# Score products of a pair of units issued in two halves, with the weight transposes of the preceding unit between them

## The chip, the core and the metric

The kernel runs on one core of a Trainium2 chip. The metric is the device time of one execution in microseconds (us); three runs of the kernel before gave a median of 644.97 us (644.82 to 645.6). One more execution was profiled, and all rows below come from it.

A core has five engines that run their own instruction queues and meet through semaphores: TensorE (PE in the rows; PEld is its weight load), VectorE (DVE), ScalarE (ACT), GpSimd (POOL) and SyncE (SP), which here only issues DMAs. Each queue is in order.

## The reference

Three stages follow each other. This case changes the first one alone.

1. Attention over 4 batches, 8 heads of 64, 512 local tokens and 32 global ones. A local query sees the 32 global keys and the local keys within 32 positions; a global query sees all.

```python
s_ll = np.where(np.abs(pos[:, None] - pos[None, :]) <= 32, scale * q_l @ k_l.T, -1e9)
a_l  = sm(np.concatenate([scale * q_l @ k_g.T, s_ll], axis=-1))   # row-wise softmax
out_l = a_l @ np.concatenate([v_g, v_l])
out_g = sm(scale * q_g @ k_all.T) @ v_all
```

2. A mixture of 8 experts (512 to 1024 to 512) over the 2304 resulting tokens, one expert a token. The choice is serial along a sequence: a token takes its own best expert, or the one of the token before, by a gate computed from the token.
3. A gated feed-forward layer with a convolution of three taps along the sequence.

## The kernel before, in words

The attention runs over 32 units `n`, in the order batch `b`, quarter `i` of the local queries (128 tokens), half `g` of the heads (4 heads). An even unit and the odd one behind it are a pair: they share the batch and the tokens and differ in the half of the heads. Code is written out by hand in program order (`manual_schedule`): each engine executes what the Python loop emits for it, in that order. The steps of a unit are spread over several turns of the loop (`Attn.run`, L459 on):

- `s_mm` (L247), at even units only, for both units of the pair: eight mask products (L259, bf16), then 32 score products (L267, in the order of the four heads `hp`, four windows `c`, two halves). They use a quarter-width, half-height part of the array each (64x32), and each is two matmuls in the trace, 64 a pair. The results are two tiles `sp`, one for each unit.
- `softmax` (L271): a reduction to the row's minimum on DVE (L275, `nm`), then four exponentials on ACT (L278, `pr`). The reduction needs the whole `sp` of its unit.
- `pt` (L281), one turn later: four 128x128 transposes of `pr` on PE (L286, `ptp`, a PSUM tile of the ring `tr`), and a copy on ACT (L288, `pts`), which frees the PSUM tile.
- `pv_norm` (L448), two turns later: 32 products with V on PE (L300; 128x32), and at odd units the division by the sum on DVE and the store.

The names of the tiles around them: `trp` (L173) are transposes of the next batch's keys and queries, `trx` (L319) transposes of the finished tokens for the logits, `sa`, `sb`, `ptg`, `og` (L368, L389, L399) the same steps for the global queries. All names beginning with `r_` belong to the routing of the experts, which VectorE works on from unit 21 on. `trp`, `ptp`, `trx`, `ptg` and `sb` share the three PSUM buffers `tr`: a fourth one waits until the first has been copied away.

In a turn of the loop the emission is: `s_mm` (even units), `softmax`, the transposes and copies for the next batch, `pt` of the unit before, `x_t`, `pv_norm` of the unit two before, logits, the steps of the global queries. Behind the attention comes the tail of the routing (to about 180 us), then the experts and the feed-forward stage, each with its products queued on PE in program order.

Of the kernel before, what the change touches and what calls it, by code (L numbers as in the profile page):

```python
# [87 lines left out]
class Attn:  # L88
# [158 lines left out]
    def s_mm(self, n):  # L247
        b, i, _ = n
        nc = self.nc
        qT, kT = self.qT[b % 2], self.kT[b % 2]  # L250
        sp = [self.psS.tile([P, 4, P], F32, tag="S", name="sp") for _ in range(2)]
        rows = [slice(64 * g, 64 * g + 64) for g in range(2)]
        for c in range(4):
            u = 4 * i + c
            edge = u in (0, 15)
            t = u // 15 if edge else (u - 1) % 3
            for g, r in enumerate(rows):
                o = 64 * g + 32 * edge
                nc.tensor.matmul(sp[g][32 * c:32 * c + 32], self.identb[r, o:o + 32],  # L259
                                 self.masks[r, t, None, :].to_broadcast([64, 4, P]), start=True, stop=False)  # L260
        for hp in range(4):
            for c in range(4):
                u = 4 * i + c
                v = u - 1
                s0 = 4 * (v // 3) + (0, 2, 3)[v % 3] + 1
                for g, r in enumerate(rows):
                    nc.tensor.matmul(sp[g][32 * c:32 * c + 32, hp, :], qT[r, hp, 32 * u:32 * u + 32],  # L267
                                     kT[r, hp, s0:s0 + 4, :], start=False, stop=hp == 3)
        return sp

    def softmax(self, n, sp):  # L271
        b, i, g = n
# [137 lines left out]
    def run(self):  # L410
        nc = self.nc
        units = [(b, i, g) for b in range(B) for i in range(4) for g in range(2)]
        N = len(units)
        pr, pts, ops, xs, xts, gst = {}, {}, {}, {}, {}, {}
        self.alloc(0)
        for a in range(4):
            self.load_qk(0, 1, a)
            self.load_qk(0, 0, a)
        self.load_gn(0)
        self.load_g(0)  # L420
        self.load_v(0, range(2))
        self.alloc(1)
        for a in range(N_K1):
            self.load_qk(1, 1, a)
        self.warm(NWARM)
        arr = {1: nc.vector.tensor_copy, 0: nc.scalar.copy}
        for a in range(5):
            for t in (1, 0):
                if a < 4:
                    self.arrange_a(0, t, a, arr[t])  # L430
            for t in (1, 0):
                if a > 0:
                    self.tr_all(0, t, a - 1, "tr")
        self.tr_g(0)
        self.warm(NWARM_G)
        eng = {"a": nc.scalar.copy, "p": nc.gpsimd.tensor_copy, "v": nc.vector.tensor_copy}
        glob, vcopy = self.copy_v(0, (0, 2), (0, 1), (0, 2), True)
        for e, j in zip(E_VG, glob):
            eng[e](*j)
        self.load_v(0, range(2, 6))  # L440
        self.copy_v(0, (2, 4), (1, 3), (2, 4))
        self.copy_v(0, (4, 6), (3, 5), (4, 6))
        for a in range(N_K1, 4):
            self.load_qk(1, 1, a)
        self.load_qk(1, 0)
        self.load_g(1)

        def pv_norm(n):  # L448
            b, i, g = units[n]
            if g == 0:  # L450
                ops[0] = self.ps1.tile([P, 2, 512], F32, tag="O", name="op")
            self.pv(units[n], pts.pop(n), ops[0])
            if g == 1:
                xf = self.norm(ops[0])
                t0 = b * S + SG + 128 * i
                nc.sync.dma_start(self.x_dram[t0:t0 + 128, :], xf)
                xs[n] = xf

        for n in range(N):  # L459
            b, i, g = units[n]  # L460
            m = n % 8
            self.n = n
            if g == 0:
                sps = self.s_mm(units[n])
            sp = sps[g]
            if n == N - 1:
                pts[n - 1] = self.pt(units[n - 1], pr.pop(n - 1))
            tr = []
            if b + 1 < B:
                pc = nc.gpsimd.tensor_copy  # L470
                ars, trs, mg = ARS[b > 0], TRS[b > 0], MG[b > 0]
                tr = list(trs.get(m, ()))
            if n in Q_EARLY:
                while tr and tr[0] > 3:
                    self.tr_all(b + 1, 0, tr.pop(0) - 4)
            pr[n] = self.softmax(units[n], sp)
            if n == 1:
                for e, j in zip(E_VC, vcopy):
                    eng[e](*j)
            next(self.late, None)  # L480
            self.hook(n, 0)
            if b + 1 < B:
                if m == mg:
                    self.tr_g(b + 1)
                for st in tr:
                    self.tr_all(b + 1, 1 - st // 4, st % 4)
                for st in ars.get(m, ()):
                    self.arrange_a(b + 1, 1 - st // 4, st % 4, pc if b else nc.scalar.copy)
                for a in LD_Q[b].get(m, ()):
                    self.load_qk(b + 1, 0, a)  # L490
                if 2 <= m < 5:
                    self.load_v(b + 1, range(2 * m - 4, 2 * m - 2))
                if m == (5 if b == 0 else 2) and b + 2 < B:
                    self.alloc(b + 2)
                    self.load_g(b + 2)
                if b + 2 < B:
                    for t in (1, 0):
                        for a in PF[b > 0][t].get(m, ()):
                            self.load_qk(b + 2, t, a)
                if m == 3:  # L500
                    self.copy_v(b + 1, (0, 3), (0, 3), (0, 3))
                if m == 4:
                    self.copy_v(b + 1, (3, 6), (3, 5), (3, 6))
            self.copy_some(V_JOBS[min(b, 2)].get(m, 0))
            self.warm(WARM.get(n, 0))
            if 0 < n < N - 1:
                pts[n - 1] = self.pt(units[n - 1], pr.pop(n - 1))
            if n - 3 in xs:
                b, i, g = units[n - 3]
                xts[i] = self.x_t(xs.pop(n - 3))  # L510
            if n >= 2:
                pv_norm(n - 2)
            if 0 <= n - 4 and (n - 4) % 8 == 7:
                self.logits([xts[i] for i in range(4)], units[n - 4][0])
            if n == 19:
                self.logits([self.x_t(xg, 64)], 4, 64)
            if 0 <= n - 5 < N - 1 and (n - 5) % 8 == 7:
                self.evac(units[n - 5][0], self.ps, "tr")
                if n == 20:
                    self.evac(4, self.ps, "tr", 64)  # L520
            b, i, g = units[n]
            m = n % 8
            for gg in range(2):
                st = m - ((3 + 2 * gg) if b == 0 else (2 if b < 3 else 0) + 3 * gg)
                if st == 0:
                    gst[gg] = self.sg_softmax(b, gg, *self.sg_mm(b, gg))
                if st == 1:
                    gst[gg, "p"] = self.sg_pt(gst[gg])
                if st == 2:
                    self.sg_pv(b, gg, gst[gg, "p"])  # L530
            if n == 8:
                self.c2.close()
            if n == 17:
                xg = self.load_xg(range(2))
            if b == 3 and m == 6:
                xg = self.load_xg(range(B))
            self.hook(n, 1)
        hk = iter(range(N, N + 9))
        pv_norm(N - 2)
        xt = self.x_t(xg)  # L540
        pts[N - 1] = self.pt(units[N - 1], pr.pop(N - 1))
        self.hook(next(hk), 1)
        xts[2] = self.x_t(xs.pop(N - 3))
        pv_norm(N - 1)
        self.hook(next(hk), 1)
        self.logits([xt], 4)
        self.hook(next(hk), 1)
        xts[3] = self.x_t(xs.pop(N - 1))
        self.evac(4, self.ps, "tr")
        t = self.ps.tile([P, P], F32, tag="tr", name="lgp")  # L550
        self.logit_mm(t, xts, range(3))
        self.hook(next(hk), 1)
        self.logit_mm(t, xts, (3,))
        self.logit_out(t, 3)
        self.hook(next(hk), 1)
        self.evac(3, self.ps, "tr")
# [1166 lines left out]
```

## Time and profile before

| | |
|---|---|
| median of 3 runs | 644.97 us |
| the profiled execution | 645.35 us, of which the span from the first to the last instruction is 643.6 us |
| PE busy | 604.7 us, 94% of the span |
| PEld / DVE / ACT / POOL busy | 508.0 / 418.8 / 320.9 / 174.7 us |
| granted TensorE clock | 0.995 of 2.4 GHz over the span |
| the units of the attention | about 12 to 142 us of the span |

The busy times are sums over the whole span. In the views of a stretch, a row of the timeline is a run of like instructions: its start, its length, the engine, the line, the operation, the tiles with their shapes, how many (x), and in brackets how long the engine had been idle before and what ended that. "issue" stands for an idle time for which the trace shows no other engine. Matmuls are pipelined: the length of one matmul (0.27 us) is longer than the distance between the starts of two.

### The profile page before, as it was taken

The page shows a single profiled execution, that of the slowest core. Times are in us where ns is not written, and L with a number is a line of the kernel's source. Part 1 is how long each engine was busy: PE and PEld are TensorE (multiplying, and loading weights), DVE is VectorE, ACT ScalarE, POOL GpSimd, SP SyncE. Part 2 cuts the span into 40 slices and gives each one's busy share as a digit, 9 for nine tenths or more (in the row PEclk, how much of TensorE's full clock was granted, in tenths as well). Part 3 has the DMA queues.
Part 4 walks back from the last instruction along what each step waited for, and adds up shares of the span by engine and source line. Part 5 has one row for each costly group of instructions (what it writes and reads, how often), then busy time and mean ns, then how long its engine had stood idle before and what let it go on. Part 6 is the DMA issues. An engine that isn't in the chain of part 4 may idle for free. (4 is left out here: it accounts for less than half of the span.)

```text
span 643.6 us, 15270 instructions
## 1 busy us (share of the span) xinstructions
PE 604.7 (94%) x5898; PEld 508.0 (79%) x5898; DVE 418.8 (65%) x874; ACT 320.9 (50%) x629; POOL 174.7 (27%) x226
## 2 busy tenths in 40 slices
PE   8888898888999999999999999987999999999997
PEld 7666676665778888888888888857998898898986
DVE  7877577958836676875778677586893393393340
ACT  4754555573225546352454634664874374373331
POOL 7664810070212232423222251000042042300200
PEclk9999999999999999999999999997999999999999
DMA  9999668652158454953545494023101201000001
GB/s 226 217 244 236 177 142 209 240 168 75 55 201 314 140 182 171 344 207 132 211 143 184 145 347 157 16 86 88 31 20 49 68 16 50 34 1 34 34 34 49
DMA packets 60089, 88.12 MB, mean 137 GB/s; under 512 B 25710, under 2 KB 34182, under 8 KB 59976
## 3 DMA queue, kind: packets, MB, share of 16 engines
q1 hardware_dynamic: 56488, 76.83, 38.3%
q0 software_dynamic: 3520, 10.23, 4.6%
q8 instruction: 48, 0.79, 0.5%
q14 instruction: 33, 0.27, 0.1%
HBM read 125.87 MB, written 15.79 MB: 220 GB/s over the span
## 5 line engine op out<-in xcount | busy, mean ns | idle before, releaser
L1433 DVE SCALAR_TENSOR_TENSOR fc<-f_hp,cw,fc 128x544 f32<-128x544 f32 (+2 forms) x66 | 51.4, 778 | 71.5 <-ACT fc L1431 70.0
L1027 DVE TENSOR_TENSOR wl<-ws,wh 128x512 fp32r<-128x512 f32 (+1 forms) x92 | 71.8, 848 | 5.3 <-ACT wh L1026 5.2
L1106 PE MATMUL yp<-wh,gh 128*128 128x512 f32 x176 | 71.0, 404 | 1.1 <-ACTq L1277 0.9
L1106 PE MATMUL yp<-wl,gh 128*128 128x512 f32 x176 | 69.0, 392 | 0.7 <-DVEq L1277 0.7
L1106 PE MATMUL yp<-wh,gl 128*128 128x512 f32 x176 | 69.1, 393 | 0.0
L1026 ACT CAST wh<-ws 128x512 fp32r<-128x512 f32 (+1 forms) x96 | 66.1, 779 | 0.0
L1255 ACT ACTIVATE hs<-hp 128x512 f32<-128x512 f32 x44 | 24.3, 595 | 74.2 <-PE hp L1090 74.1
L1090 PE MATMUL hp<-wh,xh 128*128 128x512 f32 x176 | 58.6, 405 | 0.7 <-ACT xh L1079 0.7
L1090 PE MATMUL hp<-wl,xh 128*128 128x512 f32 x176 | 56.2, 392 | 0.0
L1090 PE MATMUL hp<-wh,xl 128*128 128x512 f32 x176 | 56.0, 391 | 0.0
L1491 PE MATMUL f<-wh,fh 128*128 128x512 f32 (+1 forms) x144 | 55.5, 385 | 0.0
L1491 PE MATMUL f<-wl,fh 128*128 128x512 f32 (+1 forms) x144 | 55.0, 382 | 0.0
L1491 PE MATMUL f<-wh,fl 128*128 128x512 f32 (+1 forms) x144 | 55.0, 382 | 0.0
L1063 POOL DMA_INDIRECT y_dram<-ys,sidx x22 | 24.6, 1118 | 105.7 <-ACT ys L1259 88.9
L1083 DVE TENSOR_TENSOR gl<-hlp,gh 128x512 fp32r<-128x512 f32 x44 | 28.4, 686 | 32.4 <-ACT gh L1079 32.3
L278 ACT ACTIVATE pr<-sp,nm 128x128 f32<-128x128 f32 x128 | 36.6, 376 | 25.7 <-DVE nm L275 25.7
L999 POOL TENSOR_TENSOR wf<-wf,fx 128x512 int32<-128x512 int32 x16 | 20.8, 1303 | 100.9 <-DVE fx L998 100.9
L1259 ACT COPY ys<-yp 128x512 f32<-128x512 f32 x22 | 12.9, 587 | 61.2 <-PE yp L1106 56.5
L1051 POOL DMA_INDIRECT xs<-x_dram,gidx x22 | 27.5, 1249 | 45.5 <-ACT pr L278 34.0
L1106 PEld LDWEIGHTS yp<-wh,gh 128*128 128x128 f32 x176 | 33.1, 188 | 7.7 <-ACTq L1277 1.1
L1090 PEld LDWEIGHTS hp<-wl,xh 128*128 128x128 f32 x176 | 32.9, 188 | 7.8 <-DVE wl L1027 0.9
L1106 PEld LDWEIGHTS yp<-wh,gl 128*128 128x128 f32 x176 | 33.0, 188 | 7.6 <-DVE gl L1083 0.6
(357 smaller groups left out, 1492.5 us busy)
## 6 DMA issues: line engine op xcount, KB each, us to landing
ws<-in_moe_w_dram SPq DMA_DIRECT2D x42, 2048.0 KB
fx<-y_dram SPq DMA_DIRECT2D x17, 256.0 KB
raw<-in_k_l_dram SPq DMA_DIRECT2D x16, 256.0 KB
x_dram<-x SPq DMA_DIRECT2D x16, 256.0 KB
fx<-in_moe_w_in_dram SPq DMA_DIRECT2D x8, 512.0 KB
fx<-in_moe_w_out_dram SPq DMA_DIRECT2D x8, 512.0 KB
out_dram<-fy SPq DMA_DIRECT2D x16, 256.0 KB
VA<-in_v_l_dram SPq DMA_DIRECT2D x20, 192.0 KB
```

The lines of the kernel that those rows point to most:

```text
L278: nc.scalar.activation(pr[:, hp, :], sp[:, hp, :], AF.Exp, bias=nm[:, hp:hp + 1], scale=-1.0)
L999: nc.gpsimd.tensor_tensor(a, a, lo, ALU.add)
L1026: (cp.tensor_copy if cp else self.nc.scalar.copy)(h, src[n][:, k, :])
L1027: eng.tensor_tensor(l, src[n][:, k, :], h.bitcast(F32), ALU.subtract)
L1051: self.nc.gpsimd.indirect_dma_start(out=xs, out_offset=None, in_=self.x_dram[0:n, :], in_offset=bass.IndirectOffsetOnAxis(ap=self.rt.gidx[ ...
L1063: self.nc.gpsimd.indirect_dma_start(out=self.y_dram[:, :], out_offset=bass.IndirectOffsetOnAxis(ap=self.rt.sidx[:, s:s + 1], axis=0), in_= ...
L1083: self.nc.vector.tensor_tensor(hl[1][:, a:a + 4], t, hl[0][:, a:a + 4].bitcast(F32), ALU.subtract)
L1090: self.nc.tensor.matmul(hp[c], a[:, k, :], b[:, 512 * c:512 * c + 512], start=k == 0 and m == 0, stop=k == NKC - 1 and m == 2)
L1106: self.nc.tensor.matmul(yp, a[:, k, :], b, start=k == 0 and m == 0, stop=k == NFC - 1 and m == 2)
L1255: self.nc.scalar.activation(hs[:, 512 * c:512 * c + 512], hp[c], AF.Relu)
L1433: nc.vector.scalar_tensor_tensor(c[:, a:b], hp[:, a + t:b + t], self.cw[:, t, f:f + 1], c[:, a:b], ALU.mult, ALU.add)
L1491: self.nc.tensor.matmul(yp[:, cs], x[:, c], w[:, cs], start=f == 0 and n == 0, stop=f == NFC - 1 and n == 2)
```

## The change

`s_mm` becomes a generator. It stops once, behind the score products of the first two of four heads (`hp` 0 and 1), and then goes on. At an even unit `n` other than 0, `run` emits `pt(n - 1)` at that stop: the four transposes and, on ACT, the copy of `pts`. The place further down where `pt(n - 1)` stood is now reached by odd units only. This moves 15 of the 31 calls of `pt`, those of the odd units 1 to 29; the arithmetic is the same.

```diff
         for hp in range(4):
+            if hp == 2:
+                yield sp
             for c in range(4):
                 u = 4 * i + c
...
-        return sp
...
             if g == 0:
-                sps = self.s_mm(units[n])
+                mm = self.s_mm(units[n])
+                sps = next(mm)
+                if n:
+                    pts[n - 1] = self.pt(units[n - 1], pr.pop(n - 1))
+                for _ in mm:
+                    pass
             sp = sps[g]
...
-            if 0 < n < N - 1:
+            if g and n < N - 1:
                 pts[n - 1] = self.pt(units[n - 1], pr.pop(n - 1))
```

The queue of PE at unit 20, from the last mask product to the first product with V, before (32 score products there are 64 matmuls in the trace):

```order
L259 MATMUL sp<-masks,identb 32x512
L267 MATMUL sp<-kT_138,qT_140 32x128 x32
L173 MATMUL trp<-ident,nat 128x128 x4
L286 MATMUL ptp<-ident,pr 128x128 x4
L319 MATMUL trx<-ident,x 128x128 x4
L300 MATMUL op<-VA_142,pts 32x65
```

and in the changed kernel, whose lines behind L260 stand one or two further down:

```order
L259 MATMUL sp<-masks,identb 32x512
L269 MATMUL sp<-kT_138,qT_140 32x128 x16
L287 MATMUL ptp<-ident,pr 128x128 x4
L269 MATMUL sp<-kT_138,qT_140 32x128 x16
L173 MATMUL trp<-ident,nat 128x128 x4
L320 MATMUL trx<-ident,x 128x128 x4
L301 MATMUL op<-VA_142,pts 32x65
```

The four transposes `ptp` moved from behind `trp` into the middle of the score products. The queue of ACT from unit 16's exponentials (`pr_1804`) to unit 18's, before (the numbers are those of the tiles; `sp_1760`, `sp_1761` and `sp_1903` are the scores of units 16, 17 and 18):

```order
L278 ACTIVATE pr_1804<-sp_1760,nm_1802 128x128 x4
L288 COPY pts_1826<-ptp_1821 128x512
L278 ACTIVATE pr_1854<-sp_1761,nm_1852 128x128 x4
L288 COPY pts_1875<-ptp_1870 128x512
L278 ACTIVATE pr_1947<-sp_1903,nm_1945 128x128 x4
L288 COPY pts_1966<-ptp_1961 128x512
```

and in the changed kernel:

```order
L289 COPY pts_1791<-ptp_1786 128x512
L279 ACTIVATE pr_1811<-sp_1760,nm_1809 128x128 x4
L279 ACTIVATE pr_1854<-sp_1761,nm_1852 128x128 x4
L289 COPY pts_1875<-ptp_1870 128x512
L289 COPY pts_1934<-ptp_1929 128x512
L279 ACTIVATE pr_1954<-sp_1903,nm_1952 128x128 x4
```

The copy of unit 15's `pts` now stands ahead of unit 16's exponentials and that of unit 17's ahead of unit 18's, where they stood behind them; the copy of unit 16's (`pts_1875`) stays behind unit 17's.

## Rows read from the trace of the kernel before

**Rows 1.** Busy us by stretch: PE, PEld, DVE, ACT, POOL; clock, DMA share, GB/s.

```profile
12.00:142.00 130.00, 110.36 (x3146) 85.47 (x3144) 97.68 (x287) 76.13 (x212) 56.83 (x61) 1.00 0.78 203
142.00:185.00 43.00, 37.98 (x260) 29.27 (x258) 31.77 (x124) 12.05 (x22) 8.44 (x7) 1.00 0.28 86
185.00:438.00 253.00, 246.28 (x1202) 202.32 (x1200) 172.90 (x279) 126.44 (x215) 66.05 (x60) 1.00 0.52 187
438.00:643.00 205.00, 200.74 (x1252) 182.21 (x1252) 108.39 (x157) 100.84 (x172) 33.58 (x62) 0.99 0.12 39
```

**Rows 2.** Waits of PE, 12 to 142 us: line, releaser, total, times, longest.

```profile
PE sp L267 <- issue: 4.5, 4, 1.4
PE ptp L286 <- issue: 2.2, 2, 1.6
PE op L300 <- issue: 1.9, 2, 1.0
...
PE trp L173 <- ACT nat L166: 1.3, 1, 1.3
```

**Rows 3.** Timeline of PE, unit 20: start and length (us), engine, line, tiles, count.

```profile
93.63 0.41 PE L259 MATMUL sp<-masks,identb 64*32 64x512 bf16 x8
93.86 1.13 PE L267 MATMUL sp<-kT,qT 64*32 64x128 f32 x64
94.92 0.66 PE L173 MATMUL trp<-ident,nat 128*128 128x128 f32 x4
95.41 0.60 PE L286 MATMUL ptp<-ident,pr 128*128 128x128 f32 x4
95.85 0.60 PE L319 MATMUL trx<-ident,x 128*128 128x128 f32 x4
96.38 0.24 PE L300 MATMUL op<-VA,pts 128*32 128x65 f32 x1
```

**Rows 4.** Timeline of the weight loads there.

```profile
93.66 1.06 PEld L267 LDWEIGHTS sp<-kT,qT 64*32 64x32 f32 x64
94.92 0.42 PEld L173 LDWEIGHTS trp<-ident,nat 128*128 128x128 f32 x4 [0.20 <-issue]
95.31 0.47 PEld L286 LDWEIGHTS ptp<-ident,pr 128*128 128x128 f32 x4
```

**Rows 5.** Groups of instructions, 12 to 142 us: busy us, mean ns, idle before.

```profile
L275 DVE TENSOR_REDUCE nm<-sp 128x4 f32<-128x512 f32 x32 | 21.8, 685 | 8.7 <-PE sp L267 8.4
...
L267 PE MATMUL sp<-kT,qT 64*32 64x128 f32 x1024 | 20.6, 272 | 4.5 <-issue 4.5
```

**Rows 6.** Timeline, units 2 and 3.

```profile
17.99 0.69 DVE L275 TENSOR_REDUCE nm<-sp 128x4 f32<-128x512 f32 x1 [0.66 <-PE sp L267]
...
20.42 0.66 PE L173 MATMUL trp<-ident,nat 128*128 128x128 f32 x4 [1.28 <-ACT nat L166]
```

**Rows 7.** Timeline, unit 7.

```profile
39.92 0.63 ACT L288 COPY pts<-ptp 128x512 f32<-128x512 f32 x1
...
40.61 0.66 PE L173 MATMUL trp<-ident,nat 128*128 128x128 f32 x4 [0.34 <-ACT pts L288]
```

**Rows 8.** Timeline, unit 22.

```profile
106.84 0.67 DVE L321 COPY xt<-trx 128x512 f32<-128x512 f32 x1
...
107.57 0.44 PE L389 MATMUL ptg<-ident,pg 128*128 128x128 f32 x2 [0.78 <-DVE xt L321]
```

**Rows 9.** Timeline, units 25 and 26.

```profile
117.59 1.14 ACT L278 ACTIVATE pr<-sp,nm 128x128 f32<-128x128 f32 x4 [0.43 <-DVE nm L275]
...
118.05 1.13 PE L267 MATMUL sp<-kT,qT 64*32 64x128 f32 x64
```

**Rows 10.** Timeline, unit 26, further on.

```profile
121.56 0.86 PE L399 MATMUL og<-VA,pgt 128*32 128x65 f32 x48
...
122.07 0.68 DVE L321 COPY xt<-trx 128x512 f32<-128x512 f32 x1
...
122.90 0.63 PE L286 MATMUL ptp<-ident,pr 128*128 128x128 f32 x4 [0.48 <-DVE gsm L402]
```

## The prediction, made before the changed kernel ran

> **What bounds the kernel now.** Read the busy time by stretch first [rows 1]. In the attention, from 12 to 142 us, PE is busy 110.4 of 130 us, DVE 97.7, ACT 76.1; from 185 us to the end PE is busy 447.0 of 458. So behind the attention PE is the limit, each of its products queued behind the one before, and a delay at the end of the attention goes to the end of the kernel nearly whole. In the attention PE is the busiest engine but not full: 20 us are idle, and there the question is what ended each idle time. That is the second view, the waits of PE [rows 2]. The largest kinds are "issue": 4.5 us within the score products, 2.2 within the weight transposes, 1.9 within the products with V, eight waits of about 1 us in all (8.6 us) for which no other engine answers. The waits for ACT or DVE are 0.2 to 1.3 us each and of many kinds. No wait of PE for the copy of `pts` or for the exponentials recurs pair by pair; what the change would relieve is therefore little. The third view is the timeline of a plain pair [rows 3, 4], for what it costs PE to go from one kind of product to the other. The granted clock is 1.00, the 2.4 GHz level, in the whole attention [rows 1], so no term is due to the clock.
>
> **The change part by part.** *The two added switches.* At unit 20, PE goes from the 64x32 score products to the 128x128 transposes, and from these to the 128x32 products with V [rows 3]. The score products start at 93.86; the row is 1.13 long and one matmul is 0.27 [rows 5], so the last of 64 starts at 94.72, one every 0.014. The first transpose starts at 94.92, 0.20 later. The first group of four takes 0.49 to the start of the next (94.92 to 95.41), the second 0.44 (95.41 to 95.85): 0.05 goes to being first. The third takes 0.53 to the first product with V (95.85 to 96.38): 0.09 goes to being last. The weight loads say the same: the first load of the transposes begins 0.20 after the last of the scores has ended, the second group's just behind the first's [rows 4].
>
> In the changed kernel the group `ptp` stands alone between two halves of score products. Its insertion costs 0.20 to enter, less the 0.01 of an ordinary step there, and 0.44 + 0.05 + 0.09 for the group: 0.77 us. At its old place it goes, and there it stood among transposes: 0.44 less. The net is 0.33 us of PE a pair, and 15 pairs make 5.0 us. The eight mask products are not touched, and no instruction is added or removed on any engine; no DMA is moved, neither on SP's queue nor on POOL's.
>
> Two pages of the Trainium skill disagree on such a place. TensorE: Matmul & The Clock Gate (Part 3, packing small matmuls) says that PE pulls a weight load ahead of matmuls still in flight when its rows of the array or the spare weight buffer are free; TensorEngine Tiling (Array Packing) (Key Properties) says that changing the tiling mode drains the engine. By the first the 5.0 would be near nothing, by the second it stands. The trace sides with the second at this boundary: the load waits those 0.20 us.
>
> *What waits for the scores.* Within `s_mm` the second half ends 0.77 later than before, so DVE's reduction of the even unit starts up to 0.77 later, not 0.33. DVE waited for the scores 9 times, 8.4 us in all [rows 5], so this is often felt by DVE. PE feels it only if something in the chain returns to PE without slack. It does at unit 2: the reduction waits for the scores (0.66), behind it come the exponentials and, on ACT, the arranging of the next keys, for which PE waits 1.28 [rows 6]. There the pair costs 0.77, that is 0.44 more. Elsewhere the even unit's exponentials have the time of a turn before PE transposes them.
>
> *The added wait.* `ptp` of an odd unit now meets PE early, with half of the scores queued behind it. The tightest place is unit 26: unit 25's exponentials end at 117.59 + 1.14 = 118.73, and half of the scores that start at 118.05 are through at about 118.48, plus 0.20 for the switch, 118.68 [rows 9]. That is a wait of 0.05, with a semaphore 0.1. At the other pairs the exponentials are done before.
>
> *What goes, and what absorbs.* The copy of `pts` now stands ahead of the even unit's exponentials on ACT, in time in which ACT waits for the reduction. At unit 7 PE waits 0.34 for the copy of unit 5, which frees a buffer of the ring [rows 7]; done ahead of the exponentials of unit 6, that wait goes: -0.34. At unit 22 PE waits 0.78 for a copy that DVE reaches in its own order behind routing work [rows 8]; PE's 0.33 there lies inside that wait: -0.33. At unit 26 it waits 0.48 for DVE, which has just finished another copy (122.07 + 0.68 = 122.75) when the product it needs ends at 122.42 [rows 10]; about 0.2 of the 0.33 is absorbed.
>
> *The "issue" waits.* How a break among score products changes them, no row shows. From below: four of the eight lie within score products, and if the 0.77 of a break, with few instructions in it, shortens each by that much, 3.1 us go. From above: one more such wait adds 1.2. I take none, because two of the eight lie within these transposes themselves, where PE's queue is as thin as in the break [rows 2].
>
> *The sum.* 5.0 + 0.4 + 0.1 - 0.3 - 0.3 - 0.2 = 4.7; with the unrounded terms 4.95 + 0.44 + 0.1 - 0.34 - 0.33 - 0.2 = 4.6 us, which I use. The profiled execution took 645.35 us (span 643.6 and 1.75 around it), so this one would take about 650.0; it is 0.4 above the median of the runs, and against the median of 644.97 the forecast is 649.6. From 142 to 185 us PE is idle for 5.0 us [rows 1], behind the last logits and the routing; that work follows PE's own last products of the attention, so I let it absorb nothing.
>
> **The rivals.** *The switches are hidden.* PE's weight loads for the other form run under the last products of the half, and the group costs the same 0.44 at both places. Then the 5.0 goes, the other terms (-0.3) stay, and the time is 644.6. For it: inside one form the loads do overlap, the second group's begins before the first's matmuls end [rows 3, 4]. Against it: the 0.20 at the boundary. The tail absorbing 4.6 of its 5.0 us idle would look the same. This is also the rule of the first page named above.
>
> *The instruction waits go, and the kernel is faster.* PE's "issue" waits are 8.6 us [rows 2]. If they come from instructions arriving too slowly for dense runs, a break in every pair lets them catch up. With all gone the change is 4.6 - 8.6 = -4.0, 641.0 us. It decides from 4.6 of the 8.6 on, and is faster by more than 0.2% from 5.9. Against it: only 4.5 lie in the score products, and my lower bound for these is 3.1, which leaves +1.5.
>
> *The lateness of the scores is passed on in each pair.* If the chain of DVE's reduction, ACT's exponentials and PE's next transposes sets the pace, each pair costs 0.77: 15 times makes 11.6, 656.6 us. For it: DVE's 8.4 us of waiting for scores [rows 5]. Against it: PE's waits name these exponentials nowhere as a recurring kind, and DVE is idle for 32 of the 130 us.
>
> That the change does not move what it says is excluded: the queue of PE shows the transposes between two halves of 16 score products, and ACT's the copy ahead of the exponentials.
>
> **How the numbers follow.** My forecast 0.76, with a range of its own from 647.5 (two thirds of the 3.1 gone) to 651.5 (one more wait, and a second place like unit 2); hidden switches 0.10; instruction waits gone 0.08; lateness passed on 0.06. The range for 8 in 10 is 645.0 to 652.0: it leaves out the faster case, the one beyond 652, and about half of the hidden switches. Below 0.2%, or 1.3 us, this kernel's runs cannot tell a change from none. Faster by more: 0.08, the second rival. Within: 0.10 for hidden switches and 0.02 from the low end of my forecast, 0.12. Slower: 0.80.
>
> **What would show it.** In the timeline of unit 20 of the changed kernel: about 32 score matmuls, 0.20, four transposes, 0.20, 32 score matmuls, and from the first mask product to the first product with V 0.33 us more than the 2.75 of now [rows 3]. The total of waits of PE from the same point of the attention to the same point should be about as now, with the one at unit 7 gone and those at units 22 and 26 shorter. The end of the attention should come some 4.6 us later and all behind it be shifted by that. The prediction is wrong if the boundaries inside `s_mm` cost less than 0.2 together, if the "issue" waits change by more than 2 us, or if the shift at 185 us is gone by the end.

## The result, and the profile after

The changed kernel took 649.83 us (median of 20 executions, 647.49 to 653.63); the kernel before, run between them on the same chip, took 646.73 (20 executions, 644.82 to 656.85). The ratio is 1.0057 with an interval of 1.004 to 1.0073: slower by 3.7 us (by the medians alone 3.1), where 4.6 were forecast. The profiled execution is the longest of the 20, 653.63 us with a span of 651.9; a second profiled execution of the same kernel, called the quiet one below (`a2` in the runs), took 648.36 with a span of 646.6. Both are used, and it matters which: the quiet one had the 2.4 GHz level throughout the attention, as [rows 1] had.

The timeline of PE at unit 20 of the changed kernel, which answers to [rows 3]:

```profile
97.76 0.41 PE L259 MATMUL sp<-masks,identb 64*32 64x512 bf16 x8
97.98 0.64 PE L269 MATMUL sp<-kT,qT 64*32 64x128 f32 x32
98.55 0.66 PE L287 MATMUL ptp<-ident,pr 128*128 128x128 f32 x4
99.14 0.67 PE L269 MATMUL sp<-kT,qT 64*32 64x128 f32 x32
99.73 0.66 PE L173 MATMUL trp<-ident,nat 128*128 128x128 f32 x4
100.22 0.60 PE L320 MATMUL trx<-ident,x 128*128 128x128 f32 x4
100.75 0.24 PE L301 MATMUL op<-VA,pts 128*32 128x65 f32 x1
```

From the first mask product to the first product with V it is 2.99 us, 0.24 more than the 2.75 of [rows 3]. The boundary is there: the last score matmul of the first half starts at 97.98 + 0.64 - 0.27 = 98.35, the first transpose 0.20 later. The transposes take 0.59 to the start of the second half (98.55 to 99.14). Both were forecast so. What was not: the halves take 0.37 and 0.40 from their first start to their last, together 0.77, where the whole took 0.86. Taken over all 15 pairs, with PE's waits in between left out, the median of this difference is 0.25 us in each of four profiled executions of the changed kernel. Fifteen times this is 3.75 us of boundaries, not 4.95; in the quiet execution the 15 differences add up to 3.8.

Busy time by stretch (PE, PEld, DVE, ACT, POOL; clock, DMA share, GB/s), first of the profiled execution, then of the quiet one:

```profile
12.00:142.00 130.00, 108.97 (x2957) 80.36 (x2949) 95.39 (x278) 70.86 (x198) 51.34 (x59) 0.99 0.77 191
```

```profile
12.00:142.00 130.00, 111.87 (x3080) 82.56 (x3077) 97.30 (x282) 74.08 (x205) 54.64 (x60) 1.00 0.78 198
```

The mean of 0.99 in the first hides a fall that is shown below. The waits of PE between 12 and 150 us (total, times, longest) of the profiled execution, beside [rows 2]:

```profile
PE sp L269 <- issue: 7.1, 4, 2.5
PE trp L173 <- ACT nat L166: 1.9, 1, 1.9
PE hlp L1084 <- DMA xs<-x_dram,gidx: 1.7, 1, 1.7
PE trx L320 <- ACT pg L381: 1.6, 1, 1.6
...
PE ptp L287 <- DVE qT L241: 0.9, 1, 0.9
...
PE op L301 <- issue: 0.6, 1, 0.6
...
PE ptp L287 <- ACT pts L289: 0.6, 1, 0.6
```

and of the quiet one:

```profile
PE sp L269 <- issue: 4.8, 5, 1.3
...
PE hlp L1084 <- DMA xs<-x_dram,gidx: 1.6, 1, 1.6
...
PE op L301 <- issue: 0.6, 1, 0.6
```

The two waits of "issue" within the transposes `ptp` of [rows 2] have left the transposes in both. The longer one has not left the kernel: in the pair of unit 28 it now stands within the score products. First the kernel before, then the changed one in the third set's execution:

```profile
130.15 0.55 PE L286 MATMUL ptp<-ident,pr 128*128 128x128 f32 x3 [1.61 <-issue]
```

```profile
134.07 0.64 PE L269 MATMUL sp<-kT,qT 64*32 64x128 f32 x5 [2.08 <-issue]
```

In the profiled execution it is 2.48 at the same place, in the quiet one 1.12. The last section says at which instructions these waits stand. `hlp` are transposes of the rows that the experts gather by DMA; the wait for this DMA is new in these two executions. All waits of PE in the view sum to 22.0 and 18.7 us, against 19.2 of the kernel before.

Behind the attention nothing was absorbed. The first product of the experts began at 142.81 us before, at 150.51 in the profiled execution and at 146.15 in the quiet one: 7.7 and 3.3 later. The spans ended 8.3 and 3.0 later.

### The profile page after: what moved, and what is told of

Same layout as the page of the kernel before. It is cut to its first block, busy times and chain, and to the rows that moved or that the text cites. A ratio compares the mean times of both kernels' runs of the same rounds, so it can differ in the third digit from the quotient of the medians.

```text
span 651.9 us, 15264 instructions
## 1 busy us (share of the span) xinstructions
PE 610.5 (94%) x5898; PEld 506.4 (78%) x5898; DVE 421.1 (65%) x874; ACT 322.1 (49%) x629; POOL 175.6 (27%) x226
## 5 line engine op out<-in xcount | busy, mean ns | idle before, releaser
L1112 PEld LDWEIGHTS yp<-wl,gh 128*128 128x128 f32 x176 | 33.6, 191 | 7.4 <-DVEq L1283 1.0
```

Source lines behind the costliest of these rows:

```text
L1112: self.nc.tensor.matmul(yp, a[:, k, :], b, start=k == 0 and m == 0, stop=k == NFC - 1 and m == 2)
```

## The experiments

All ratios are to the kernel before, executed between on the same chip, with a 95% interval. Its medians in the three sets were 648.2, 647.18 and 648.39, so 0.1% is 0.65 us throughout.

### The first set: the break moved, doubled, emptied

The changed kernel once more, unedited:

> The changed kernel once more, since its first profile held a wait of PE for instructions of 2.1 us in unit 14, 3.5 us at the lower clock level behind it and a wait of 2.5 us in unit 28, all of which may be of that one execution. If the two added switches in each of 15 pairs are the cost (theory 1), every pair shows 0.79 us from the 32nd to the 33rd score matmul again, the time is 3.5 to 4.8 us above the kernel before, and the long waits fall elsewhere or not at all. If the longer time is due to instruction waits and a lower clock that the change brings about (theory 2), the profile shows the clock fall again in unit 14, the granted clock stays under 0.993, and the time of the attention without these places is as before.

649.35 us, ratio 1.002 (1.0003 to 1.0036): slower, by 1.3 us only. This interval and the 1.004 to 1.0073 of the result exclude each other, with the same two kernels in both. Sets differ by more than the intervals say, so kernels are best compared within one set.

The transposes directly behind the whole score products, with no added boundary. This has everything of the change but the break: the transposes and the copy of `pts` stand ahead of the even unit's exponentials. The edit is shown against the changed kernel, and `s_mm` is again the function that it was.

```diff
-                mm = self.s_mm(units[n])
-                sps = next(mm)
+                sps = self.s_mm(units[n])
                 if n:
                     pts[n - 1] = self.pt(units[n - 1], pr.pop(n - 1))
-                for _ in mm:
-                    pass
```

> The transposes of the odd unit stand directly behind the whole of the score products, ahead of the transposes for the next batch: the order on ScalarE is that of the changed kernel, and TensorE has no more switches than before. Theory 1 (the added switches cost): no slower than before, 0 to 0.6 us faster for the copy that is done earlier. Theory 2 (instruction waits and clock): as the changed kernel's, if they come from the earlier transposes and copies, so 2 to 4 us slower than before. Theory 3 (the later scores hold up VectorE and ScalarE): no slower than before, since the scores end as early as before.

646.73 us, ratio 0.9983 (0.9956 to 1.001): no difference from before, and 2.6 us below the changed kernel's 649.35 of the same set. PE at unit 20:

```profile
92.54 0.41 PE L259 MATMUL sp<-masks,identb 64*32 64x512 bf16 x8
92.77 1.13 PE L267 MATMUL sp<-kT,qT 64*32 64x128 f32 x64
93.83 0.66 PE L286 MATMUL ptp<-ident,pr 128*128 128x128 f32 x4
94.32 0.60 PE L173 MATMUL trp<-ident,nat 128*128 128x128 f32 x4
...
95.29 0.24 PE L300 MATMUL op<-VA,pts 128*32 128x65 f32 x1
```

The pair takes the 2.75 us of [rows 3] again. Moving the transposes earlier costs nothing that these runs can tell; breaking the score products for them does.

Two breaks, with two of the four transposes in each (the line of the break is shown; the calls follow the pattern of the next cut):

```diff
-            if hp == 2:
+            if hp in (1, 3):
                 yield sp
```

> The score products are broken twice, behind the first and behind the third head, with two of the four transposes in each break: four added switches in a pair instead of two. Theory 1: 2 x (0.20 - 0.01 + 0.05 + 0.09) = 0.66 us a pair, 9.9 in 15 pairs, less 0.3 to 0.6 for the same small terms: 9.3 to 9.6 us above the kernel before, that is 4.7 above the changed kernel. Theory 3 (the scores end 1.10 us later than before, and this is passed on): 16 us. If a break lets instructions catch up, less than theory 1, down to 4 us.

653.04 us, ratio 1.0084 (1.0062 to 1.0107), where 9.3 to 9.6 us were expected and 5.4 came.

One break with a single transpose in it, the other three behind the second half. `pt_parts` is `pt` as a generator that stops ahead of the transposes named in its last argument:

```diff
                 sps = next(mm)
-                if n:
-                    pts[n - 1] = self.pt(units[n - 1], pr.pop(n - 1))
+                gp = self.pt_parts(units[n - 1], pr.pop(n - 1), (1,)) if n else iter(())
+                while True:
+                    try:
+                        next(gp)
...
+                    next(mm, None)
```

> One of the four transposes stands between the halves, the other three directly behind the second half. Theory 1 (the price is that of the boundary, not of what is inside): 0.20 to enter and 0.20 to leave, less 0.01 and the 0.11 of the transpose at its other place: 0.28 us a pair, 4.2 in 15, less 0.3: some 3.9 us above the kernel before, close to the changed kernel. Theory 3 (the time by which the scores end later, here 0.39 us instead of 0.77): about half of what the changed kernel costs, 2 us.

650.21 us, ratio 1.0034 (1.0009 to 1.0058). PE at unit 20, first with one transpose inside:

```profile
96.90 0.41 PE L259 MATMUL sp<-masks,identb 64*32 64x512 bf16 x8
97.12 0.64 PE L269 MATMUL sp<-kT,qT 64*32 64x128 f32 x32
97.69 0.33 PE L296 MATMUL ptp<-ident,pr 128*128 128x128 f32 x1
97.95 0.67 PE L269 MATMUL sp<-kT,qT 64*32 64x128 f32 x32
98.55 0.55 PE L296 MATMUL ptp<-ident,pr 128*128 128x128 f32 x3
...
99.90 0.24 PE L310 MATMUL op<-VA,pts 128*32 128x65 f32 x1
```

then with two breaks (of the third set's execution):

```profile
96.62 0.41 PE L259 MATMUL sp<-masks,identb 64*32 64x512 bf16 x8
96.85 0.40 PE L269 MATMUL sp<-kT,qT 64*32 64x128 f32 x16
97.18 0.44 PE L296 MATMUL ptp<-ident,pr 128*128 128x128 f32 x2
97.55 0.67 PE L269 MATMUL sp<-kT,qT 64*32 64x128 f32 x32
98.14 0.44 PE L296 MATMUL ptp<-ident,pr 128*128 128x128 f32 x2
98.51 0.45 PE L269 MATMUL sp<-kT,qT 64*32 64x128 f32 x16
...
99.91 0.24 PE L310 MATMUL op<-VA,pts 128*32 128x65 f32 x1
```

From mask to V these take 3.00 and 3.29 us: 0.25 and 0.54 over the 2.75. Over the 15 pairs the medians are 0.25 to 0.27 and 0.55. So the price on PE belongs to the break and not to what stands in it. The single transpose delays the second half by 0.46 (97.69 to 97.95, 0.26, plus 0.20 to enter) instead of 0.79, and its time is that of the changed kernel within the intervals. Were the lateness paid in each pair, this would be 6.9 us and the change 11.9. Measured are 2.2 for the single transpose, with 3.8 at the upper end of its interval, and 3.7 for the change, with 4.7 at the upper end.

### The second set: is there a better version, and how quiet is the kernel before

The kernel before and the changed kernel, one profile each:

> The kernel before, profiled once more. If the lower clock level behind unit 14 in the changed kernel's two profiles is the change's work (theory 2), the clock stays at 1.00 from 12 to 142 us here, as in the first profile of the kernel before, and the waits for instructions are again about 8.6 us in eight places of 0.6 to 1.6. If it is a matter of the execution, a fall of the clock and waits of 2 us may show here as well.

> The changed kernel, profiled a third time. From the 32nd to the 33rd score matmul 0.79 us in every undisturbed pair; the waits for instructions within 2 us of the 8.6 of the kernel before (8.5 and 7.5 in the two profiles so far). If breaks let instructions catch up, they are below 8.6 here too. If the fall of the clock in unit 14 is the change's, it is here again.

652.24 us for the kernel before, in this execution, and 648.36 for the changed one: single executions spread over more than the change is worth. What sets them apart is the clock, in the last section.

The version without a break again:

> The transposes of the odd unit directly behind the whole of the score products, a second set of rounds: 0.9983 of the kernel before in the first, with an interval from 0.9956 to 1.001. If the earlier copy and the other order of the transposes gain something (some 1 us instead of the 0.3 to 0.6 of the prediction), it is 1 to 2 us faster again; if not, within 0.6 us.

648.28 us, ratio 1.0012 (0.9986 to 1.0038); with the first, both intervals hold 1. On top of it the transposes of the logits (`evac`, L346) ahead of the products with V:

```diff
+            if 0 <= n - 5 < N - 1 and (n - 5) % 8 == 7:
+                self.evac(units[n - 5][0], self.ps, "tr")
...
             if n >= 2:
                 pv_norm(n - 2)
...
-            if 0 <= n - 5 < N - 1 and (n - 5) % 8 == 7:
-                self.evac(units[n - 5][0], self.ps, "tr")
...
```

> As the kernel with the transposes behind the score products, and the transposes of the logits (units 12, 13, 20, 21 and 28, 29: those of line 346) stand ahead of the products with V, next to other transposes, instead of behind them. It takes away two switches in each of three places, at 12, 20 and 28. Theory 1: 0.3 us each, 0.9 us faster than the kernel without it, in all 1.5 to 2.5 us faster than the kernel before. If switches cost nothing of the time at the end: no difference to the kernel without it.

647.63 us, ratio 0.9997 (0.9968 to 1.0026). (The edit acts at units 12, 20 and 28 alone, not at the odd ones that the text above lists.) PE around unit 20:

```profile
95.29 0.60 PE L319 MATMUL trx<-ident,x 128*128 128x128 f32 x4
...
96.39 0.18 PE L346 MATMUL r_t<-ident,lgt 32*64 32x32 f32 x1 [0.31 <-DVE kT L183]
97.00 0.86 PE L399 MATMUL og<-VA,pgt 128*32 128x65 f32 x48
```

At unit 20 the boundary that was saved came back as a wait for a copy of DVE: from `trx` to `og` it is 1.71 us here and 1.61 without the edit. The intervals are too wide to tell the 0.9 us that were expected of this edit. No version beat the kernel before measurably.

### The third set: both sizes again, and the opposite direction

> The kernel before, profiled a third time, for how far the waits for instructions from 12 to 150 us differ between executions (8.6 and 10.3 us so far; 8.5, 7.5 and 5.7 in the changed kernel, 4.4 in the one with two breaks). If the breaks shorten these waits, this one lies above 8 again; if they only differ from execution to execution, it may lie anywhere from 4 to 10.

> The changed kernel, a further set of rounds, since 1.0057 and 1.002 of the kernel before do not agree well. Its pairs cost TensorE 0.25 us each without the waits, 3.75 in 15 (not the 0.33 and 5.0 of the prediction). If all of it arrives at the end: 1.0058. If part is taken back by shorter waits, as the second set says: 1.002 to 1.004.

> Two breaks in the score products, a second set of rounds and a second profile. Its pairs cost 0.55 us each, 8.25 in 15. If all of it arrives: 1.0128 of the kernel before; the first set gave 1.0084. If breaks shorten the waits for instructions, these are again near 4.4 us here and the time again 2 to 4 us under the full price.

649.48 us for the one execution of the kernel before. The changed kernel: 652.3, ratio 1.0058 (1.0035 to 1.0081). Two breaks: 652.55, ratio 1.0083 (1.0054 to 1.0113). Both repeat the first results.

Last, fewer boundaries than before: the transposes of both units of a pair behind the next pair's scores, and the products with V of both units together; the calls of `pt` at odd units go.

```diff
+                for k in (n - 2, n - 1) if n else ():
+                    pts[k] = self.pt(units[k], pr.pop(k))
...
-            if n >= 2:
-                pv_norm(n - 2)
+            for k in (n - 2, n - 1) if n and n % 2 == 0 else ():
+                pv_norm(k)
```

> The transposes of both units of a pair stand together behind the score products of the next pair, and the products with V of both behind them, so that a pair has one stretch of transposes and one of products with V instead of two. At odd units without transposes for the next batch (four pairs) two switches go, some 0.33 us each pair; at the eleven others one goes, some 0.15. Theory 1: 4 x 0.33 + 11 x 0.15 = 3.0 us faster than the kernel before, 0.9953 of it. If a stretch of odd units without these products leaves TensorE waiting for VectorE and ScalarE instead, the gain is lost or turned: 0 to 5 us slower.

661.38 us, ratio 1.0205 (1.0172 to 1.0237): 13 us slower, outside both ranges that were expected. Its waits of PE, 12 to 160 us:

```profile
PE sp L267 <- issue: 5.1, 3, 2.1
PE lgp L334 <- issue: 3.9, 1, 3.9
PE trx L319 <- DMA xgt<-x_dram: 2.7, 1, 2.7
PE og L399 <- DVE pgt L390: 2.4, 1, 2.4
PE ptg L389 <- ACT pg L379: 1.9, 1, 1.9
```

Work that lay behind the even unit's products with V now stands bare: three waits for DVE, ACT and a DMA of 1.9 to 2.7 us, and one of 3.9. All waits sum to 27.3 us up to 160, and in five places the granted clock falls to the 1.2 GHz level, 11.9 us by the sum of the last section. Fewer boundaries are no gain where they uncover waits.

## Why the prediction came out, step by step

**The added switches** are the cause, as forecast: without the break the cost is gone (0.9983 and 1.0012), with two it is 1.0084 and 1.0083, with one transpose inside it stays (1.0034). The sharpest comparison is within the first set: 646.73 without the break, 649.35 with it, 653.04 with two. The distance from the 32nd score matmul to the 33rd was forecast as 0.78. It is 0.79 in 11 of the 15 pairs of the quiet execution, 0.85 to 0.92 in three, and 1.44 at unit 26 with its wait. On this boundary the rule of TensorEngine Tiling (Array Packing) (Key Properties) in the Trainium skill, that a change of the tiling mode drains the engine, agrees with the trace, 0.20 us at each entry. The term as a whole was mis-sized: 0.33 a pair was forecast, 0.25 measured. The sum let the boundary replace one step of 0.01, the mean of a row that it read as even. The trace's single starts show that the row is not even: at unit 20 of the kernel before, the first 32 score matmuls start in groups of eight, 0.003 to 0.004 apart within most of a group and 0.086 from one group to the next, and the 33rd starts 0.07 behind the 32nd. The break stands at that step and takes its place, which makes 0.05 to 0.06 of the 0.08. The rest is the second half, which takes 0.40 from its first start to its last where it took 0.43. Fifteen times 0.08 is the 1.2 us by which the term was too high.

**The "issue" waits** were taken as unchanged, with bounds of -3.1 and +1.2. In the four profiled executions of the changed kernel they are 8.5, 7.5, 5.7 and 7.3 us, in the three of the kernel before 8.6, 10.3 and 10.1, with two breaks 4.4 and 4.0, with one transpose inside 6.0; in the three of the versions without an added break, though, 8.5, 5.9 and 5.0. That they shrink with breaks fits these numbers but is not shown, as versions without a break have executions nearly as low. The sign was on the side of my lower bound. By the means, 7.25 against 9.67, the change is 2.4 us, beyond the 2 that I had named as a sign of being wrong; the single executions overlap, so it stays open whether the change did it.

**The scores later at unit 2:** forecast +0.44, measured +0.64. DVE's reduction waits 1.40 for the scores there, and PE's next transposes (L173) wait 1.92 for ACT, where [rows 6] had 0.66 and 1.28. Without the waits the pair itself costs only 0.10 here, so together 0.74, where 0.77 was forecast. The row of DVE:

```profile
17.99 0.69 DVE L276 TENSOR_REDUCE nm<-sp 128x4 f32<-128x512 f32 x1 [1.40 <-PE sp L269]
```

**The added wait at unit 26:** forecast 0.1 for the exponentials, measured 0.59, and for something else:

```profile
123.25 0.60 ACT L289 COPY pts<-ptp 128x512 f32<-128x512 f32 x1
...
123.91 0.66 PE L287 MATMUL ptp<-ident,pr 128*128 128x128 f32 x4 [0.59 <-ACT pts L289]
```

PE waits for the end of the copy at 123.85, which frees the ring buffer that the new transposes need; this copy stands on ACT behind unit 25's exponentials. I had looked only at the operand and not at the buffer.

**What goes:** the 0.34 of [rows 7] is gone and so is the 0.48 of [rows 10]; the 0.78 of [rows 8] is down to 0.31. These three are as forecast. In their place stand waits that I had not named: the 1.7 and 1.6 us of `hlp` for its gather, which the other two executions of the changed kernel have as 0.2 and not at all; `trx` at unit 4 for ACT's `pg`, 1.6 and 1.5 us, but 0.33, 0.96 and none in the three executions of the kernel before; `ptp` for DVE's copy of queries, 0.9 and 0.4; and `og` for DVE's copy of keys, 0.6. The 0.9 of `ptp` for DVE's copy of keys at unit 4 is no new wait: before, `trp` waited 0.94 for it there.

**The sum.** Boundaries 3.75, the change in all waits of PE (18.7 - 19.2), -0.5: 3.25 us. The quiet execution's first expert product came 3.3 later and its span ended 3.0 later. There the budget closes. The forecast of 4.6 is too high by its switch term, 4.95 for 3.75. That the waits come out near the forecast's -0.3 is luck: the -0.5 is 2.9 us less of "issue" and 2.4 more of waits for other engines and DMAs, and the forecast took the first as unchanged and named few of the second.

**The medians** say the same with less sharpness. The three comparisons give 0.57, 0.20 and 0.58%, a mean of 2.9 us; 3.75 us would be 0.58%. Two of them have it in their interval; the first set's, up to 1.0036, lies below it. Whether one break costs all of its boundaries at the end therefore stays open. Two breaks do not: 8.25 us would be 1.27%, above both intervals (up to 1.0107 and 1.0113), and some 5.4 are measured. A part of the difference is the median, since the 15 pairs of the first profile, all at the full clock, add up to 7.7. Where the other 2 us go stays open; PE's waits are lower in its two profiles (16.8 and 15.9 us against 19.2), but two executions do not settle that.

**The rivals.** Hidden switches: refuted by the 0.20 at every boundary and by the version without a break. Instruction waits gone and a faster kernel: the direction was perhaps right, the size is too small to change the sign. Lateness passed on in each pair, 11.6 us: refuted by the total, and by the single transpose inside, which makes the scores less late and costs PE the same. DVE does wait longer for scores, 14.0 us in the quiet execution against the 8.4 of [rows 5]. No wait of PE for the exponentials recurs from pair to pair because of it; whether the new waits of PE for DVE's copies and for the gather come from it is not shown. The tail absorbed nothing, as taken.

## What to carry to other kernels

Inserting a group of another tile shape between matmuls of one shape costs its boundaries each time, however much or little stands in the group; read it as the difference between the starts across one boundary in the trace of before, and read the step that already stands at the place of the break, not the mean of the row. When a transpose is moved earlier, follow its output buffer back to the copy that frees it, not only its operand. And before a change of half a per cent is judged by one profile, sum PE's waits and the time at the lower clock in each execution, since these alone move a kernel by more. Compare kernels within one set of runs.

## What was not expected of the hardware

The clock. In 11 of the 14 profiled executions, of both kernels and of the versions, TensorE's granted clock falls to 0.50, the 1.2 GHz level, for 3 to 4 us, sometimes about 7, within the attention, behind an idle time of PE or in the middle of one. In the profiled execution of the changed kernel, the wait and then the stretches (the clock is third from the end):

```profile
73.02 0.89 PE L269 MATMUL sp<-kT,qT 64*32 64x128 f32 x27 [2.08 <-issue]
```

```profile
73.00:74.00 1.00, 0.98 (x28) 0.60 (x29) 0.00 (x0) 0.17 (x1) 0.94 (x2) 0.65 0.94 289
74.00:75.00 1.00, 1.00 (x12) 0.67 (x20) 0.00 (x0) 0.00 (x0) 0.94 (x2) 0.50 1.14 388
```

and in the kernel before, in the second set:

```profile
66.77 0.24 PE L300 MATMUL op<-VB,pts 128*32 128x65 f32 x1 [2.46 <-issue]
```

```profile
67.00:68.00 1.00, 1.00 (x55) 0.86 (x49) 0.20 (x1) 0.00 (x0) 0.94 (x2) 1.00 1.11 282
68.00:69.00 1.00, 1.00 (x17) 0.91 (x6) 0.70 (x4) 0.00 (x0) 1.00 (x1) 0.58 1.04 213
69.00:70.00 1.00, 1.00 (x9) 0.67 (x8) 0.85 (x6) 0.78 (x3) 0.96 (x2) 0.50 0.90 216
```

So the change is not needed for it, and [rows 1], where the clock was 1.00 throughout, came from an execution that had no fall. A wait that the trace calls "issue" is then paid twice, as idle time and as slow products behind it. Not every such wait is: the 2.48 us of the profiled execution that end at 136.12 are followed by no fall. The time lost to it can be summed as the length of each stretch of 2 us times what its clock lacks of 1. With that, and with the waits, the shifts of the first expert product (from 142.81) are worked out for each execution, in us:

| execution | PE's waits less 19.2 | lost at the lower clock | boundaries | sum | measured shift |
|---|---|---|---|---|---|
| before, second set | +1.7 | 5.1 | 0 | 6.8 | 5.6 |
| before, third set | +0.8 | 3.4 | 0 | 4.2 | 4.2 |
| changed, profiled | +2.8 | 1.7 | 3.75 | 8.3 | 7.7 |
| changed, first set | -1.2 | 3.4 | 3.75 | 6.0 | 6.2 |
| changed, quiet | -0.5 | 0 | 3.75 | 3.3 | 3.3 |
| changed, third set | -0.6 | 2.7 | 3.75 | 5.9 | 6.8 |
| two breaks, first set | -2.4 | 0 | 8.25 | 5.9 | 4.9 |
| two breaks, third set | -3.3 | 1.7 | 8.25 | 6.7 | 6.1 |
| one transpose inside | -2.5 | 5.1 | 3.9 | 6.5 | 5.2 |
| no added break, first set | -0.1 | 1.7 | 0 | 1.6 | 0.7 |
| no added break, second set | -1.0 | 5.1 | 0 | 4.1 | 2.3 |
| the same with `evac` ahead | -2.1 | 3.4 | 0 | 1.3 | -0.9 |

The sums meet the measured shifts within 1.2 us in the first eight rows; in the last four they are 0.9 to 2.2 too high. All three executions with 5.1 us at the lower clock have sums that are 1.2 to 1.8 too high, so that column is rather an upper figure. What PE does ahead of 12 us is in no column either, and the first mask product of the attention starts anywhere from 11.2 to 14.1 us. The version with joined units is left out, as its boundaries were not measured. The column of the clock, 0 to 5.1 us, is about as large as the effect in question, and it fits this that 644.97, the median of three, lies at the low end of the 644.82 to 656.85 that the kernel before took later.

The places of the "issue" waits. They are the same in all 14 profiled executions, whatever the kernel. Number the records of the program's instructions on PE from 0 on: matmuls, weight loads and those of PE's sequencer. Of 98 such waits in the attention, 89 end at instruction 1218, 1730, 1986, 2498, 2754, 3266, 5058, 5314, 5570 or 5826, or at the one before. All these numbers lie a multiple of 256 apart, and the 89 waits make 98.1 of the 101.4 us. Of the 212 other waits of PE there, two end at such a number of the same spacing. Their lengths differ between executions of one kernel, from nothing to 2.6 us, and 3.9 in the version with joined units. So these waits belong to the count of instructions and not to the kind of product: another order only puts another product at that count, as at unit 28 above, where instruction 5826 was a transpose and is now a score product. It points to a delivery of the instructions in blocks of 256; what makes one delivery later than another is not shown.

One thing more may belong to the change. At unit 2 the wait for ACT, 1.92 us in the changed kernel, is followed by a fall in one execution of the changed kernel, in the first set:

```profile
20.95 1.11 PE L173 MATMUL trp<-ident,nat 128*128 128x128 f32 x4 [1.92 <-ACT nat L166]
```

```profile
20.00:21.00 1.00, 0.04 (x1) 0.05 (x1) 1.00 (x2) 1.00 (x4) 0.94 (x2) 0.92 0.94 212
21.00:22.00 1.00, 1.00 (x5) 1.00 (x6) 0.97 (x3) 1.00 (x4) 0.94 (x2) 0.50 0.83 181
```

and in one execution each of the versions with two breaks and with one transpose inside (where the wait is 1.63); in the other four executions with a break the wait of 1.92 is followed by none. Nor is one there in the three profiles of the kernel before, or in the three without an added break, two of which have a wait of 1.63 too. Three of seven against none of six suggests that the lengthened wait sometimes costs a fall of about 2 us; it does not show it.
